# Decode attention of two caches on one core: the loads and units of the windowed cache, from four heads in 16 KB rows to eight heads in 32 KB rows

## The chip, the core and the metric

One core of one Trainium2 chip runs the kernel as one program. The metric is the device time in microseconds, the median of three runs. Beside it stands one execution that the hardware profiler recorded; its span runs from the first to the last instruction, and the durations in this document are those of that execution. The engines are called as in the profile: PE (matrix multiplication; PEld its weight loads), DVE (vector), ACT (scalar functions), POOL, and SP, whose instruction queue issues the loads. The loads themselves are carried out by the core's 16 DMA engines.

## What is computed

Two independent attention layers, A and B, each for one token with 32 query heads over 16 cached heads of 128 elements. B attends to all 8,192 cached keys, A only to the last 2,048 of them. Each has a query projection before and an output projection behind, and the two results stand side by side in the output.

```python
def _A_ref(x, k_cache, v_cache, wq, wo):
    W = min(4096, max(256, Sk // 4))          # 2048 of Sk = 8192; B takes all Sk
    rep = Hq // Hkv                            # 32 // 16
    q = (x @ wq).reshape(B, Sq, Hq, Dh).transpose(0, 2, 1, 3)
    k = jnp.repeat(k_cache[:, :, Sk - W:, :], rep, axis=1)
    v = jnp.repeat(v_cache[:, :, Sk - W:, :], rep, axis=1)
    scores = jnp.einsum("bhqd,bhkd->bhqk", q, k) * (Dh ** -0.5)
    p = _softmax(scores, axis=-1)
    o = jnp.einsum("bhqk,bhkd->bhqd", p, v)
    return o.transpose(0, 2, 1, 3).reshape(B, Sq, Hq * Dh) @ wo
return jnp.concatenate([a, b], axis=-1)
```

All data are bfloat16. K and V of A are 8.4 MB each, of B 33.6 MB each; with wq and wo the kernel reads 102.76 MB.

## The kernel before

**Units.** The work runs in units of four cached heads (eight query heads): four units of A, then four of B, numbered 0 to 7. A unit's K is one block of 128 partitions, with a row of keys in each partition: in A 64 keys (`TA`, 16 KB), in B 256 keys (64 KB, loaded in two halves). A unit is worked on in slabs of 16 keys per partition (`SLAB`, 2,048 elements): four slabs in a unit of A (`NA`), sixteen in one of B (`NB`).

**Loads.** `load_kv` builds the loads of a unit. For A the source pattern at L222 and L223 reads, outermost first, 32 pieces of a head, then four heads, then a row, so that partition 4q + h holds piece q of head h. For B the source is a plain block of 128 rows. `place` gives each load the next piece of a ring of 144 KB per partition, and makes it wait for the last use of whatever stood there: a K slab's transpose (T) or a V slab's product (V). All loads are issued by SP, in this order: part of wo, wq in four loads of 64 rows, then K of unit 0, and after it by turns K of unit i and V of unit i-1, then the rest of wo. A waiting load holds up every load behind it. Loads of K and V of A are at L224, of B at L232, of wo at L245.

**Queries.** The query projection (L312) fills eight banks; ACT copies them out in two pieces each (L328), DVE transposes them (L332) and spreads them into two zero-filled operands: `za` for A (z0, L338) and `zb` for B (z1, L343), in which a window that moves by a few columns puts each slab's scores into rows of their own.

**Inside a unit.** `turn` transposes a K slab on DVE (T, L364) into one of three buffers; `score` multiplies it on PE (S, L381: four matmuls of 512 columns, all slabs into one bank). In A four heads share a bank, and a matmul of a small mask (`mkl`, `mkr`, L373) puts a very low number where a query meets another head's keys. Then follow the row maximum (`peak`, DVE L396, turned by PE L398), its spreading (`spread`, DVE L406 and L409, PE L411), the exponential (`expo`, ACT L417 and L420), the transpose of the probabilities (`turnp`: one instruction for A into `pta`, L428; four of 32 partitions for B into `pts`, L432), the product with V (`pv`, L445: four matmuls per slab, each into its own group of 32 output columns), a copy by ACT (`take`, L452) and the sum over the four groups on PE (`fold`, L461). The program is written out so that unit i+1's transposes and scores stand between the softmax steps of unit i, and PV of unit i behind the last score of unit i+1.

**End.** The sums of the exponentials are gathered (lsel, L496 and L499), the outputs divided, and the output projection (L525) runs over wo as it lands.

Of the kernel before, what the change touches and what calls it, by code (L numbers as in the profile page):

```python
# [22 lines left out]
NB = ROW // SLAB  # L23
TA = 4 * W_A // 128
NA = TA * DH // SLAB
W0 = 2 * (NB - 1)
ZW = 128 + W0
ZA = 128 + 24
BIG = 1e30
# [70 lines left out]
def bass_concat_heads__sliding_block_cached__gqa_block_cached__decode_kernel(nc, A_x, A_k_cache, A_v_cache, A_wq, A_wo,  # L100
# [20 lines left out]

    za = nc.alloc_sbuf_tensor("za", [128, NQ, 4, ZA], BF16)

    mkl = nc.alloc_sbuf_tensor("mkl", [4, 16, 4, 2], BF16)
    mkr = nc.alloc_sbuf_tensor("mkr", [4, 128, 4], BF16)
    mx = nc.alloc_sbuf_tensor("mx", [128, 8], F32)
    mr = nc.alloc_sbuf_tensor("mr", [128, 8], F32)

    pta = nc.alloc_sbuf_tensor("pta", [128, NA, 16, 8], BF16)
    rsa = nc.alloc_sbuf_tensor("rsa", [128, NQ], F32)  # L130
    clsa = nc.alloc_sbuf_tensor("clsa", [128, 8], F32)
    mexp = nc.alloc_sbuf_tensor("mexp", [1, 128], F32)
# [79 lines left out]
    kv_at = {}  # L212
    UNITS = [(side, u) for side in "AB" for u in range(NQ)]
    NU = len(UNITS)
    nslab = [NA if side == "A" else NB for side, _ in UNITS]

    def load_kv(kind, i):
        side, u = UNITS[i]
        c = (ks if kind == "K" else vs)["AB".index(side)]
        use = "T%d.%d" if kind == "K" else "V%d.%d"  # L220
        if side == "A":
            src = bass.AP(tensor=c.tensor, offset=c.offset + (4 * u * SK + SK - W_A) * DH,  # L222
                          ap=[[TA * DH, 32], [SK * DH, 4], [1, TA * DH]])  # L223
            kv_at[kind, i] = [place(TA * DH, [use % (i, NA - 1)], lambda e, t: e.dma_start(t, src), "%s%d.0" % (kind, i))]  # L224
            return
        rows = c[0, 4 * u:4 * u + 4, :, :].rearrange("h (q t) d -> (h q) (t d)", q=32)
        n = 2 if kind == "K" or i == NU - 1 else 1
        kv_at[kind, i] = []
        for half in range(n):
            src = rows[:, half * ROW // n:(half + 1) * ROW // n]  # L230
            kv_at[kind, i].append(place(ROW // n, [use % (i, (half + 1) * NB // n - 1)],
                                        lambda e, t, src=src: e.dma_start(t, src), "%s%d.%d" % (kind, i, half)))  # L232
# [40 lines left out]
    op("pool", lambda e: e.memset(zb[:], 0.0), name="zb0")  # L273
    op("pool", lambda e: e.tensor_copy(mkr[:], view(ident, 128, 0, [[0, 128], [1, 4]], 4)), deps=["ident"], name="mkr")
    op("pool", lambda e: e.memset(pts[:], 0.0), name="pts0")
# [15 lines left out]
    for k0 in range(0, KW, 4):  # L291
        n = min(4, KW - k0)
        for P in range(2):
# [7 lines left out]
       deps=["identf"], name="clsb")  # L301
    op("dve", lambda e: e.tensor_reduce(clsa[:], view(identf, 128, 0, [[1, 8], [8, 16]]), AX.X, ALU.add),
       deps=["identf"], name="clsa")
    op("dve", lambda e: e.tensor_reduce(sel[:], view(identf, 128, 0, [[1, 32], [32, 4]]), AX.X, ALU.add),
       deps=["identf"], name="sel")
    op("dve", lambda e: e.tensor_scalar(mkl[:], view(ident, 128, 0, [[0, 16], [1, 4], [0, 2]], 4), -1.0, BIG,
                                        ALU.add, ALU.mult), deps=["ident"], name="mkl")
# [13 lines left out]
    for n in range(8):  # L321
# [15 lines left out]
    for b in range(4):  # L337
        op("dve", lambda e, b=b: e.tensor_copy(  # L338
            view(za, NQ * 4 * ZA, ZA - 128 + 32 * b, [[4 * ZA, NQ], [2 * ZA, 2], [ZA, 2], [1, 8]], 32, 32 * b),
            view(ktb, KT, 0, [[1024, NQ], [64, 2], [1, 2], [128, 8]], 32, 32 * (b % 2))),  # L340
            deps=QT + ["za0"], name="z0.%d" % b)
# [25 lines left out]
    def score(i, s):  # L367
# [3 lines left out]
        def mm(e):  # L371
            if side == "A" and s == 0:
                e.matmul(bank[:, :], lhsT=mkl[:].rearrange("p a h r -> p (a h r)"),  # L373
                         rhs=mkr[:].rearrange("p q h -> p (q h)"), start=True, stop=False)
# [26 lines left out]
    def spread(i):  # L401
        A = UNITS[i][0] == "A"
        deps = ["mT%d" % i] + (["mx%d" % (i - 1), "bc%d" % (i - 1)] if i else [])
        rows = [[1, 8], [8, 16]] if A else [[32, 4], [1, 2], [2, 16]]
        out = mr[0:1, :] if A else mr[0:1, :].rearrange("p (b r) -> p b r", r=2)
        op("dve", lambda e: e.tensor_reduce(out, view(mb, 512, 0, rows, parts=1), AX.X, ALU.max), deps=deps,  # L406
           name="mr%d" % i)
        to, of = ([[8, 16], [1, 8]], [[0, 16], [1, 8]]) if A else ([[32, 4], [2, 16], [1, 2]], [[2, 4], [0, 16], [1, 2]])
        op("dve", lambda e: e.tensor_scalar(view(mexp, 128, 0, to, parts=1), view(mr, 8, 0, of, parts=1), -SCALE, None,  # L409
                                            ALU.mult), deps=["mr%d" % i], name="mx%d" % i)  # L410
        op("pe", lambda e: e.matmul(mb[:, 128:129], lhsT=mexp[0:1, :], rhs=onesf[0:1, 0:1], start=True, stop=True),  # L411
           deps=["mx%d" % i, "ones"], name="bc%d" % i)
# [11 lines left out]
    def turnp(i):  # L424
        side, _ = UNITS[i]
        deps = ["exp%d" % i, "pts0"] + (["V%d.%d" % (i - 1, nslab[i - 1] - 1)] if i else [])
        if side == "A":
            op("dve", lambda e: e.transpose(view(pta, NA * 128, 0, [[8, 16], [128, NA], [1, 8]]), psb[:, :]),  # L428
               deps=deps, name="PT%d" % i)
        else:  # L430
            for b in range(4):
                op("dve", lambda e, b=b: e.transpose(  # L432
                    view(pts, NB * 128, 2 * b, [[8, 16], [128, NB], [1, 2]], 32, 32 * b), psb[32 * b:32 * b + 32, :]),
                   deps=deps, name="PT%d" % i if b == 3 else None)

    def pv(i, s):
        src, landed = slab("V", i, s)

        def mm(e):
            for j in range(4):  # L440
                if UNITS[i][0] == "A":
                    lhsT = pta[:, s, 4 * j:4 * j + 4, :].rearrange("p t k -> p (t k)")
                else:
                    lhsT = view(pts, NB * 128, 128 * s + 32 * j, [[1, 32]])
                ins = e.matmul(vbank[i][32 * j:32 * j + 32, :], lhsT=lhsT, rhs=src[:, 512 * j:512 * j + 512],  # L445
                               start=(s == 0), stop=(s == nslab[i] - 1))
            return ins
# [7 lines left out]
    def fold(i):  # L455
        side, u = UNITS[i]
        c, at = (1, 8 * u) if side == "A" else (0, HQ + 8 * u)

        def mm(e):
            for t in range(4):  # L460
                ins = e.matmul(ob[:, at:at + 8], lhsT=xo[:, c, 128 * t:128 * t + 128], rhs=sel[:, 8 * t:8 * t + 8],  # L461
                               start=(t == 0), stop=(t == 3))
            return ins
        op("pe", mm, deps=["xo%d" % i, "sel"], name="O%d" % i)

# [3 lines left out]
    for i in range(NU):  # L469
# [26 lines left out]
    op("dve", lambda e: e.tensor_tensor(  # L496
        lsel[:, 0, :].rearrange("p (u m) -> p u m", m=8), rsa[:, :].unsqueeze(2).to_broadcast([128, NQ, 8]),
        view(clsa, 8, 0, [[0, NQ], [1, 8]]), ALU.mult), deps=["exp%d" % (NQ - 1), "clsa"], name="lselA")
    op("dve", lambda e: e.tensor_tensor(  # L499
# [18 lines left out]
    def final(P, c):  # L518
        k0, kk = sum(NWO[P][:c]), NWO[P][c]

        def mm(e):
# [6 lines left out]
            return ins  # L528
        op("pe", mm, deps=["wo%d.%d" % (P, c), "oP", "exp%d" % (NQ - 2)], name="F%d.%d" % (P, c))

# [43 lines left out]
```

## Time and profile before

| | |
|---|---|
| median of three runs | 246.06 us (245.97 to 246.1) |
| the profiled execution | 245.95 us, span 244.6 us |
| busiest engines | PE 168.2 us, DVE 124.7 us |
| SP's DMA queue | 102.76 MB, 98.1% of 16 engines' span |
| K transposes (L364) | 80 of 1.211 us mean |
| score matmuls (L381) | 256 for B of 0.425 us mean, 64 for A of 0.448 us mean |
| PV matmuls (L445) | 256 for B of 0.546 us mean, 64 for A of 0.382 us mean |
| granted PE clock, mean | 0.847 |

The profile gives busy time per engine; a busy time near the span means that the engine has no room left. Matmuls overlap, so the mean of one is longer than the pace at which they follow each other. For the DMA engines the profile gives packets, bytes and the share of the 16 engines' time that was filled. Windows of the profile give, for a stretch of time, the busy time of PE, PEld, DVE, ACT and POOL with counts in brackets, then the granted PE clock, the share of the DMA engines and GB/s.

### The profile page before, as it was taken

To read this page: it belongs to the slowest core of one execution; us is meant where nothing else is said; L and a number is where in the kernel's file an instruction comes from. 1 tells how busy PE (TensorE), PEld (TensorE's weight loads), DVE (VectorE), ACT (ScalarE), POOL (GpSimd) and SP (SyncE) were. 2 spreads that over 40 slices of the span, in tenths; PEclk is the share of its full clock that TensorE was granted. 3 is DMA by queue.
4 is the path that set the end of the run, shared out by engine and by line. 5 is a ranking of instruction groups with operands and counts; after the bars stand their busy time and mean duration, and the time that the engine had idled before them with its cause. 6 is when DMAs were issued, how large, how long until landed. Compare 5 with 4: busy or idle time off the path is not lost.

```text
span 244.6 us, 2224 instructions
## 1 busy us (share of the span) xinstructions
PE 168.2 (69%) x952; PEld 69.5 (28%) x952; DVE 124.7 (51%) x156; ACT 21.5 (9%) x54; POOL 8.1 (3%) x15
## 2 busy tenths in 40 slices
PE   0059692977887799669736569938197976654696
PEld 0024240322444222323112323203052322321453
DVE  0040026677688998899700679930369960130200
ACT  2200052001121100200000010000010000200000
POOL 8400000000000000000000000000000000000000
PEclk9999899579999999979968767997855995757769
DMA  7999899999999999998989999989999999999994
GB/s 279 429 486 435 367 431 429 429 429 437 434 439 434 425 437 445 429 490 386 482 375 429 429 485 396 461 370 429 426 482 418 439 423 402 431 430 426 422 412 190
DMA packets 4369, 102.90 MB, mean 421 GB/s; under 512 B 516, under 2 KB 648, under 8 KB 904
## 3 DMA queue, kind: packets, MB, share of 16 engines
q1 hardware_dynamic: 4356, 102.76, 98.1%
q8 instruction: 7, 0.11, 0.2%
q14 instruction: 2, 0.02, 0.0%
q10 hardware_dynamic: 4, 0.00, 0.0%
HBM read 102.76 MB, written 0.00 MB: 420 GB/s over the span
## 4 chain that ended last, share of the span: by engine, by line
DMA 61%; PE 21%; DVE 12%; ACT 2%; issue 2%; SPq 2%; DVEq 0%
DMA ring<-in_B_v_cache_dram 39%; DMA ring<-in_B_wo_dram 12%; DMA ring<-in_B_wq_dram 10%; DVE ktb L364 9%; PE vb L445 7%; PE qb L381 5%; PE sb L312 2%; ACT psb L420 1%; DVE pta L428 1%; PE ob L461 1%; PE vb L312 1%; PE qb L312 1%; PE sb L381 1%; SPq L201 1%; PE qb L373 1%
## 5 line engine op out<-in xcount | busy, mean ns | idle before, releaser
L364 DVE STREAM_TRANSPOSE ktb<-ring 128x1024 int32<-128x1024 int32 x80 | 92.8, 1211 | 28.2 <-DMA ring<-in_B_k_cache_dram 27.1
L381 PE MATMUL sb<-ktb,zb 128*128 128x512 bf16 x256 | 73.2, 425 | 23.2 <-DVE ktb L364 20.5
L381 PEld LDWEIGHTS sb<-ktb,zb 128*128 128x128 bf16 x256 | 22.8, 104 | 70.1 <-DVE ktb L364 45.4
L445 PE MATMUL vb<-ring,pts 128*32 128x512 bf16 x256 | 23.6, 546 | 20.6 <-DMA ring<-in_B_v_cache_dram 16.5
L381 PE MATMUL qb<-ktb,za 128*128 128x512 bf16 x64 | 19.3, 448 | 2.8 <-DVE ktb L364 2.8
L445 PEld LDWEIGHTS vb<-ring,pts 128*32 128x32 bf16 x256 | 8.5, 130 | 35.2 <-DMA ring<-in_B_v_cache_dram 18.7
L452 ACT ACTIVATE xo<-vb 128x512 f32<-128x512 f32 x8 | 4.8, 597 | 130.3 <-PE vb L445 130.3
L432 DVE STREAM_TRANSPOSE pts<-psb 32x512 bf16<-32x512 bf16 x16 | 11.3, 704 | 7.7 <-ACT psb L420 7.5
L332 DVE STREAM_TRANSPOSE ktb<-qsb 128x512 int32<-128x512 int32 x4 | 2.8, 711 | 21.8 <-ACT qsb L328 21.8
L461 PEld LDWEIGHTS ob<-sel,xo 128*128 128x128 f32 x64 | 10.0, 226 | 3.4 <-ACT xo L452 2.1
L312 PE MATMUL sb<-ring,xrep 128*128 128x512 bf16 x18 | 7.3, 546 | 5.3 <-DMA ring<-in_B_wq_dram 5.3
L525 PE MATMUL qb<-ring,oP 128*1 128x256 bf16 (+1 forms) x112 | 10.2, 326 | 0.5 <-DMA ring<-in_B_wo_dram 0.5
L461 PE MATMUL ob<-sel,xo 128*128 128x8 f32 x64 | 9.3, 273 | 1.2 <-ACT xo L452 1.2
L381 PEld LDWEIGHTS qb<-ktb,za 128*128 128x128 bf16 x64 | 6.2, 109 | 13.3 <-issue 5.7
L287 PE MATMUL sb<-onesb,xint 1*128 1x128 bf16 x8 | 1.1, 307 | 11.7 <-ACT xint L283 11.7
L525 PEld LDWEIGHTS qb<-ring,oP 128*1 128x1 bf16 x112 | 5.9, 90 | 4.8 <-DMA ring<-in_B_wo_dram 1.7
L539 DVE CAST outsb<-qb 1x256 bf16<-1x256 f32 x2 | 0.8, 420 | 12.1 <-PE qb L525 12.1
L505 DVE RECIPROCAL rl<-mb 128x64 f32<-128x64 f32 x1 | 0.6, 557 | 12.3 <-PE mb L502 12.3
L295 DVE TENSOR_SCALAR xrep<-sb,par 128x256 bf16<-128x256 f32 x4 | 1.7, 477 | 10.1 <-PE sb L287 10.1
L373 PE MATMUL qb<-mkr,mkl 4*128 4x512 bf16 x4 | 1.8, 439 | 7.2 <-DVE ktb L364 7.2
L406 DVE TENSOR_REDUCE mr<-mb 1x8 f32<-1x128 f32 x8 | 1.9, 241 | 9.4 <-PE mb L398 9.4
L396 DVE TENSOR_REDUCE mx<-qb 128x1 f32<-128x512 f32 x4 | 2.8, 692 | 6.3 <-PE qb L381 6.3
(70 smaller groups left out, 86.2 us busy)
## 6 DMA issues: line engine op xcount, KB each, us to landing
ring<-in_B_k_cache_dram SPq DMA_DIRECT2D x8, 4096.0 KB, 24.1
ring<-in_A_k_cache_dram SPq DMA_DIRECT2D x4, 2048.0 KB, 32.6
ring<-in_A_v_cache_dram SPq DMA_DIRECT2D x4, 2048.0 KB, 26.2
ring<-in_B_v_cache_dram SPq DMA_DIRECT2D x2, 4096.0 KB, 23.8
ring<-in_A_wo_dram SPq DMA_DIRECT2D x1, 3456.0 KB, 21.4
ring<-in_A_wq_dram SPq DMA_DIRECT2D x1, 2560.0 KB, 19.4
ring<-in_B_wq_dram SPq DMA_DIRECT2D x1, 2560.0 KB, 24.7
ring<-in_B_wo_dram SPq DMA_DIRECT2D x1, 2448.0 KB, 26.8
```

The lines of the kernel that those rows point to most:

```text
L201: return e.dma_start(bass.AP(tensor=ring, offset=P * RING + lo, ap=[[2 * RING, 64], [1, (k1 - k0) * w]]), src)
L312: return e.matmul(banks[n][:, :], lhsT=xrep[:, k, :], rhs=wq_at[k][:, n * 512:(n + 1) * 512], start=(k == 0), stop=(k == KW - 1))
L332: op("dve", lambda e, n=n: e.transpose(ktb[:, (n - 1) * 512:(n + 1) * 512].bitcast(I32), qsb[:, n - 1:n + 1, :].rearrange("p a n -> p (a n ...
L364: op("dve", lambda e: e.transpose(kt.bitcast(I32), src.bitcast(I32)), deps=[landed] + (["S%d" % (k - NKT)] if k >= NKT else Z), name="T%d. ...
L373: e.matmul(bank[:, :], lhsT=mkl[:].rearrange("p a h r -> p (a h r)"), rhs=mkr[:].rearrange("p q h -> p (q h)"), start=True, stop=False)
L381: ins = e.matmul(bank[:, :], lhsT=lhsT, rhs=view(ktb, KT, (k % NKT) * SLAB + 64 * c + v, [[128, 16], [2, 32]]), start=(side == "B" and s = ...
L396: op("dve", lambda e: e.tensor_reduce(mx[:, 0:1], sbank[i][:, :], AX.X, ALU.max), deps=["S%d" % (k0[i] + nslab[i] - 1)] + (["mT%d" % (i - ...
L432: op("dve", lambda e, b=b: e.transpose(view(pts, NB * 128, 2 * b, [[8, 16], [128, NB], [1, 2]], 32, 32 * b), psb[32 * b:32 * b + 32, :]), ...
L445: ins = e.matmul(vbank[i][32 * j:32 * j + 32, :], lhsT=lhsT, rhs=src[:, 512 * j:512 * j + 512], start=(s == 0), stop=(s == nslab[i] - 1))
L452: op("act", lambda e: e.activation(xo[:, c, :], vbank[i][:, :], ACT.Copy), deps=["V%d.%d" % (i, nslab[i] - 1)] + (["O%d" % (i - 1)] if i e ...
L461: ins = e.matmul(ob[:, at:at + 8], lhsT=xo[:, c, 128 * t:128 * t + 128], rhs=sel[:, 8 * t:8 * t + 8], start=(t == 0), stop=(t == 3))
L525: ins = e.matmul(fb[r:r + 1, 0:hi - lo], lhsT=oP[:, P, k0 + k:k0 + k + 1], rhs=wo_at[P, c][:, k * DM + lo:k * DM + hi], start=(k0 + k == 0 ...
```

## The change

A now runs in two units of eight cached heads instead of four units of four, so there are six units. A row in a partition holds 128 keys of a head (32 KB); the source pattern reads, outermost first, eight heads, then 16 pieces, then a row, so that partition 16h + q holds piece q of head h. There are four loads of 4 MB for K and V of A instead of eight of 2 MB, and eight slabs in a unit of A. The number of K transposes, score and PV matmuls stays the same. Half of the scores of a bank are masked (two heads share a group of 32 partitions), the mask has two rows instead of four. A's probabilities are now transposed in four parts like B's, into a `pta` that POOL clears first; PV of A writes two groups of 64 columns, each group twice per slab; the fold sums over two groups with a wider selection (`sela`). On the way, z1 moves from DVE to ACT in eight small copies, and the first two banks of queries are copied out in four pieces each. The diff, cut:

```diff
-TA = 4 * W_A // 128
+HA = 8
+UA = G // HA
+TA = HA * W_A // 128
 NA = TA * DH // SLAB
...
-ZA = 128 + 24
+RA = 2 * HA // 4
+WA = RA * (NA - 1)
+ZA = 128 + WA
...
-    UNITS = [(side, u) for side in "AB" for u in range(NQ)]
+    UNITS = [(side, u) for side in "AB" for u in range(UA if side == "A" else NQ)]
...
-            src = bass.AP(tensor=c.tensor, offset=c.offset + (4 * u * SK + SK - W_A) * DH,
-                          ap=[[TA * DH, 32], [SK * DH, 4], [1, TA * DH]])
+            src = bass.AP(tensor=c.tensor, offset=c.offset + (HA * u * SK + SK - W_A) * DH,
+                          ap=[[SK * DH, HA], [TA * DH, 128 // HA], [1, TA * DH]])
...
+    op("pool", lambda e: e.memset(pta[:], 0.0), name="pta0")
...
+    op("dve", lambda e: e.tensor_reduce(sela[:], view(identf, 128, 0, [[1, 8 * HA], [8 * HA, 2]]), AX.X, ALU.add),
+       deps=["identf"], name="sela")
...
-        for h in range(2):
-            op("act", lambda e, n=n, h=h: e.activation(qsb[:, n, 256 * h:256 * h + 256],
-                                                       banks[n][:, 256 * h:256 * h + 256], ACT.Copy),
-               deps=["qmm%d" % (KW0 + n)], name="qe%d" % n if h else None)
+        cut = 128 if n < 2 else 256
+        for lo in range(0, 512, cut):
+            op("act", lambda e, n=n, lo=lo, cut=cut: e.activation(qsb[:, n, lo:lo + cut], banks[n][:, lo:lo + cut],
+                                                                  ACT.Copy),
+               deps=["qmm%d" % (KW0 + n)], name="qe%d" % n if lo + cut == 512 else None)
...
     for b in range(4):
-        op("dve", lambda e, b=b: e.tensor_copy(
-            view(zb, NQ * 4 * ZW, 32 * b + W0, [[4 * ZW, NQ], [2 * ZW, 2], [ZW, 2], [1, 2]], 32, 32 * b),
-            view(ktb, KT, b * 256, [[1024, NQ], [64, 2], [1, 2], [128, 2]], 32, 64 + 32 * (b % 2))),
-            deps=QT + ["zb0"], name="z1.%d" % b)
+        for c in range(2):
+            op("act", lambda e, b=b, c=c: e.activation(
+                view(zb, NQ * 4 * ZW, 32 * b + W0 + 2 * ZW * c, [[4 * ZW, NQ], [ZW, 2], [1, 2]], 32, 32 * b),
+                view(ktb, KT, b * 256 + 64 * c, [[1024, NQ], [1, 2], [128, 2]], 32, 64 + 32 * (b % 2)), ACT.Copy),
+                deps=QT + ["zb0"], name="z1.%d" % b if c else None)
...
                     if side == "A":
-                        lhsT = za[:, u, 2 * c + v, ZA - 128 - 8 * s:ZA - 8 * s]
+                        lhsT = za[:, u, 2 * c + v, WA - RA * s:WA - RA * s + 128]
...
-        if side == "A":
-            op("dve", lambda e: e.transpose(view(pta, NA * 128, 0, [[8, 16], [128, NA], [1, 8]]), psb[:, :]),
-               deps=deps, name="PT%d" % i)
-        else:
-            for b in range(4):
...
+        t, n, m = (pta, NA, RA) if side == "A" else (pts, NB, 2)
+        for b in range(4):
+            op("dve", lambda e, b=b: e.transpose(
+                view(t, n * 64 * m, m * b, [[4 * m, 16], [64 * m, n], [1, m]], 32, 32 * b), psb[32 * b:32 * b + 32, :]),
+               deps=deps, name="PT%d" % i if b == 3 else None)
...
-                    lhsT = pta[:, s, 4 * j:4 * j + 4, :].rearrange("p t k -> p (t k)")
+                    lhsT, w, g = pta[:, s, 4 * j:4 * j + 4, :].rearrange("p t k -> p (t k)"), 8 * HA, 2
...
-                ins = e.matmul(vbank[i][32 * j:32 * j + 32, :], lhsT=lhsT, rhs=src[:, 512 * j:512 * j + 512],
-                               start=(s == 0), stop=(s == nslab[i] - 1))
+                ins = e.matmul(vbank[i][w * (j % g):w * (j % g) + w, :], lhsT=lhsT, rhs=src[:, 512 * j:512 * j + 512],
+                               start=(s == 0 and j < g), stop=(s == nslab[i] - 1 and j >= 4 - g))
```

More of the change, by code (lines that the diff above doesn't have):

```diff
@@ L120, in bass_concat_heads__sliding_block_cached__gqa_block_cached__decode_kernel @@
     zb = nc.alloc_sbuf_tensor("zb", [128, NQ, 4, ZW], BF16)
-    za = nc.alloc_sbuf_tensor("za", [128, NQ, 4, ZA], BF16)
-    mkl = nc.alloc_sbuf_tensor("mkl", [4, 16, 4, 2], BF16)
-    mkr = nc.alloc_sbuf_tensor("mkr", [4, 128, 4], BF16)
+    za = nc.alloc_sbuf_tensor("za", [128, UA, 4, ZA], BF16)
+    mkl = nc.alloc_sbuf_tensor("mkl", [2, 32, 2, 2], BF16)
+    mkr = nc.alloc_sbuf_tensor("mkr", [2, 16, 2, 16], BF16)
     mx = nc.alloc_sbuf_tensor("mx", [128, 8], F32)
[L127 to L131, printed above, removed]
+    mr = nc.alloc_sbuf_tensor("mr", [128, 2 * HA], F32)
+    pta = nc.alloc_sbuf_tensor("pta", [128, NA, 16, 2 * HA], BF16)
+    rsa = nc.alloc_sbuf_tensor("rsa", [128, UA], F32)
+    clsa = nc.alloc_sbuf_tensor("clsa", [128, 2 * HA], F32)
     mexp = nc.alloc_sbuf_tensor("mexp", [1, 128], F32)
@@ L139, in bass_concat_heads__sliding_block_cached__gqa_block_cached__decode_kernel @@
     sel = nc.alloc_sbuf_tensor("sel", [128, 32], F32)
+    sela = nc.alloc_sbuf_tensor("sela", [128, 8 * HA], F32)
     par = nc.alloc_sbuf_tensor("par", [128, 2], F32)
@@ L273, in bass_concat_heads__sliding_block_cached__gqa_block_cached__decode_kernel @@
     op("pool", lambda e: e.memset(zb[:], 0.0), name="zb0")
-    op("pool", lambda e: e.tensor_copy(mkr[:], view(ident, 128, 0, [[0, 128], [1, 4]], 4)), deps=["ident"], name="mkr")
+    op("pool", lambda e: e.tensor_copy(mkr[:], view(ident, 128, 0, [[0, 16], [1, 2], [0, 16]], 2)), deps=["ident"],
+       name="mkr")
+    op("pool", lambda e: e.memset(pta[:], 0.0), name="pta0")
     op("pool", lambda e: e.memset(pts[:], 0.0), name="pts0")
@@ L301, in bass_concat_heads__sliding_block_cached__gqa_block_cached__decode_kernel @@
        deps=["identf"], name="clsb")
-    op("dve", lambda e: e.tensor_reduce(clsa[:], view(identf, 128, 0, [[1, 8], [8, 16]]), AX.X, ALU.add),
+    op("dve", lambda e: e.tensor_reduce(clsa[:].rearrange("p (b r) -> p b r", r=RA),
+                                        view(identf, 128, 0, [[32, 4], [1, RA], [RA, NA]]), AX.X, ALU.add),
        deps=["identf"], name="clsa")
+    op("dve", lambda e: e.tensor_reduce(sela[:], view(identf, 128, 0, [[1, 8 * HA], [8 * HA, 2]]), AX.X, ALU.add),
+       deps=["identf"], name="sela")
     op("dve", lambda e: e.tensor_reduce(sel[:], view(identf, 128, 0, [[1, 32], [32, 4]]), AX.X, ALU.add),
        deps=["identf"], name="sel")
-    op("dve", lambda e: e.tensor_scalar(mkl[:], view(ident, 128, 0, [[0, 16], [1, 4], [0, 2]], 4), -1.0, BIG,
+    op("dve", lambda e: e.tensor_scalar(mkl[:], view(ident, 128, 0, [[0, 32], [1, 2], [0, 2]], 2), -1.0, BIG,
                                         ALU.add, ALU.mult), deps=["ident"], name="mkl")
@@ L338, in bass_concat_heads__sliding_block_cached__gqa_block_cached__decode_kernel @@
         op("dve", lambda e, b=b: e.tensor_copy(
-            view(za, NQ * 4 * ZA, ZA - 128 + 32 * b, [[4 * ZA, NQ], [2 * ZA, 2], [ZA, 2], [1, 8]], 32, 32 * b),
-            view(ktb, KT, 0, [[1024, NQ], [64, 2], [1, 2], [128, 8]], 32, 32 * (b % 2))),
+            view(za, UA * 4 * ZA, WA + 32 * b, [[4 * ZA, UA], [2 * ZA, 2], [ZA, 2], [1, RA]], 32, 32 * b),
+            view(ktb, KT, RA * DH * b, [[2 * HA * DH, UA], [64, 2], [1, 2], [128, RA]], 32, 32 * (b % 2))),
             deps=QT + ["za0"], name="z0.%d" % b)
     for b in range(4):
-        op("dve", lambda e, b=b: e.tensor_copy(
-            view(zb, NQ * 4 * ZW, 32 * b + W0, [[4 * ZW, NQ], [2 * ZW, 2], [ZW, 2], [1, 2]], 32, 32 * b),
-            view(ktb, KT, b * 256, [[1024, NQ], [64, 2], [1, 2], [128, 2]], 32, 64 + 32 * (b % 2))),
-            deps=QT + ["zb0"], name="z1.%d" % b)
+        for c in range(2):
[3 more added lines that the diff above has]
+                deps=QT + ["zb0"], name="z1.%d" % b if c else None)
     Z = ["%s.%d" % (z, b) for z in ("z0", "z1") for b in range(4)]
@@ L373, in mm @@
                 e.matmul(bank[:, :], lhsT=mkl[:].rearrange("p a h r -> p (a h r)"),
-                         rhs=mkr[:].rearrange("p q h -> p (q h)"), start=True, stop=False)
+                         rhs=mkr[:].rearrange("p t h g -> p (t h g)"), start=True, stop=False)
             for c in range(2):
@@ L403, in spread @@
         deps = ["mT%d" % i] + (["mx%d" % (i - 1), "bc%d" % (i - 1)] if i else [])
-        rows = [[1, 8], [8, 16]] if A else [[32, 4], [1, 2], [2, 16]]
-        out = mr[0:1, :] if A else mr[0:1, :].rearrange("p (b r) -> p b r", r=2)
+        m, n = (RA, NA) if A else (2, NB)
+        out = mr[0:1, 0:4 * m].rearrange("p (b r) -> p b r", r=m)
+        rows = [[32, 4], [1, m], [m, n]]
         op("dve", lambda e: e.tensor_reduce(out, view(mb, 512, 0, rows, parts=1), AX.X, ALU.max), deps=deps,
            name="mr%d" % i)
-        to, of = ([[8, 16], [1, 8]], [[0, 16], [1, 8]]) if A else ([[32, 4], [2, 16], [1, 2]], [[2, 4], [0, 16], [1, 2]])
-        op("dve", lambda e: e.tensor_scalar(view(mexp, 128, 0, to, parts=1), view(mr, 8, 0, of, parts=1), -SCALE, None,
+        to, of = [[32, 4], [m, n], [1, m]], [[m, 4], [0, n], [1, m]]
+        op("dve", lambda e: e.tensor_scalar(view(mexp, 128, 0, to, parts=1), view(mr, 2 * HA, 0, of, parts=1), -SCALE, None,
                                             ALU.mult), deps=["mr%d" % i], name="mx%d" % i)
@@ L425, in turnp @@
         side, _ = UNITS[i]
-        deps = ["exp%d" % i, "pts0"] + (["V%d.%d" % (i - 1, nslab[i - 1] - 1)] if i else [])
-        if side == "A":
-            op("dve", lambda e: e.transpose(view(pta, NA * 128, 0, [[8, 16], [128, NA], [1, 8]]), psb[:, :]),
-               deps=deps, name="PT%d" % i)
-        else:
-            for b in range(4):
-                op("dve", lambda e, b=b: e.transpose(
-                    view(pts, NB * 128, 2 * b, [[8, 16], [128, NB], [1, 2]], 32, 32 * b), psb[32 * b:32 * b + 32, :]),
-                   deps=deps, name="PT%d" % i if b == 3 else None)
+        deps = ["exp%d" % i, "pts0", "pta0"] + (["V%d.%d" % (i - 1, nslab[i - 1] - 1)] if i else [])
+        t, n, m = (pta, NA, RA) if side == "A" else (pts, NB, 2)
[3 more added lines that the diff above has]
+               deps=deps, name="PT%d" % i if b == 3 else None)
     def pv(i, s):
@@ L441, in mm @@
                 if UNITS[i][0] == "A":
-                    lhsT = pta[:, s, 4 * j:4 * j + 4, :].rearrange("p t k -> p (t k)")
+                    lhsT, w, g = pta[:, s, 4 * j:4 * j + 4, :].rearrange("p t k -> p (t k)"), 8 * HA, 2
                 else:
-                    lhsT = view(pts, NB * 128, 128 * s + 32 * j, [[1, 32]])
-                ins = e.matmul(vbank[i][32 * j:32 * j + 32, :], lhsT=lhsT, rhs=src[:, 512 * j:512 * j + 512],
-                               start=(s == 0), stop=(s == nslab[i] - 1))
+                    lhsT, w, g = view(pts, NB * 128, 128 * s + 32 * j, [[1, 32]]), 32, 4
+                ins = e.matmul(vbank[i][w * (j % g):w * (j % g) + w, :], lhsT=lhsT, rhs=src[:, 512 * j:512 * j + 512],
+                               start=(s == 0 and j < g), stop=(s == nslab[i] - 1 and j >= 4 - g))
             return ins
@@ L456, in fold @@
         side, u = UNITS[i]
-        c, at = (1, 8 * u) if side == "A" else (0, HQ + 8 * u)
+        c, at, n, pick = (1, 2 * HA * u, 2 * HA, sela) if side == "A" else (0, HQ + 8 * u, 8, sel)
         def mm(e):
             for t in range(4):
-                ins = e.matmul(ob[:, at:at + 8], lhsT=xo[:, c, 128 * t:128 * t + 128], rhs=sel[:, 8 * t:8 * t + 8],
+                ins = e.matmul(ob[:, at:at + n], lhsT=xo[:, c, 128 * t:128 * t + 128], rhs=pick[:, n * t:n * t + n],
                                start=(t == 0), stop=(t == 3))
             return ins
-        op("pe", mm, deps=["xo%d" % i, "sel"], name="O%d" % i)
+        op("pe", mm, deps=["xo%d" % i, "sel", "sela"], name="O%d" % i)
     for s in range(nslab[0]):
@@ L496, in bass_concat_heads__sliding_block_cached__gqa_block_cached__decode_kernel @@
     op("dve", lambda e: e.tensor_tensor(
-        lsel[:, 0, :].rearrange("p (u m) -> p u m", m=8), rsa[:, :].unsqueeze(2).to_broadcast([128, NQ, 8]),
-        view(clsa, 8, 0, [[0, NQ], [1, 8]]), ALU.mult), deps=["exp%d" % (NQ - 1), "clsa"], name="lselA")
+        lsel[:, 0, :].rearrange("p (u m) -> p u m", m=2 * HA), rsa[:, :].unsqueeze(2).to_broadcast([128, UA, 2 * HA]),
+        view(clsa, 2 * HA, 0, [[0, UA], [1, 2 * HA]]), ALU.mult), deps=["exp%d" % (UA - 1), "clsa"], name="lselA")
     op("dve", lambda e: e.tensor_tensor(
@@ L528, in mm @@
             return ins
-        op("pe", mm, deps=["wo%d.%d" % (P, c), "oP", "exp%d" % (NQ - 2)], name="F%d.%d" % (P, c))
+        op("pe", mm, deps=["wo%d.%d" % (P, c), "oP", "exp%d" % (UA - 2)], name="F%d.%d" % (P, c))
     for P in range(2):
```

## The prediction

> **What bounds the kernel now.** I read the page from the top: busy shares and slices, then the DMA queues, then the mean rates of three stretches, then the DMA issues, and last SP's own order of time.
>
> ```profile
> PE 168.2 (69%) x952; PEld 69.5 (28%) x952; DVE 124.7 (51%) x156; ACT 21.5 (9%) x54; POOL 8.1 (3%) x15
> DMA  7999899999999999998989999989999999999994
> DMA packets 4369, 102.90 MB, mean 421 GB/s; under 512 B 516, under 2 KB 648, under 8 KB 904
> q1 hardware_dynamic: 4356, 102.76, 98.1%
> q10 hardware_dynamic: 4, 0.00, 0.0%
> ```
>
> No engine is busy over 69% of the span, while SP's queue (q1) holds the 16 DMA engines for 98.1% of it: 240.0 of 244.6 us. The only empty stretches are the start and the end. So the time is the time of a stream of 102.76 MB, and an edit to PE, DVE or ACT counts only if it starves that stream.
>
> ```profile
> 28.00:62.00 34.00, 26.16 (x105) 9.87 (x105) 19.11 (x30) 6.81 (x20) 0.00 (x0) 0.80 1.01 432
> 62.00:81.00 19.00, 15.29 (x105) 7.80 (x105) 14.32 (x19) 4.04 (x11) 0.00 (x0) 1.00 1.00 427
> 125.00:242.00 117.00, 81.48 (x552) 35.46 (x553) 49.83 (x59) 5.66 (x14) 0.00 (x0) 0.76 0.99 426
> ```
>
> The last number of each line is GB/s, the one before it the share of the DMA engines. A's K and V load in the first stretch (seven of the eight 2 MB loads), B's K in the second, V, K and wo in the third. A's 16 KB rows run at the same rate as B's 32 and 64 KB rows, 427 to 432 GB/s, or 27 GB/s per DMA engine. The trace's record of single packets gives the same as durations (means): 0.617 us for a row of 16 KB (1,024 of them, half at 0.611), 1.218 us for 32 KB, 2.423 us for 64 KB.
>
> ```profile
> ring<-in_A_k_cache_dram SPq DMA_DIRECT2D x4, 2048.0 KB, 32.6
> ring<-in_B_v_cache_dram SPq DMA_DIRECT2D x2, 4096.0 KB, 23.8
> 74.33 12.91 SPq L232 DMA_DIRECT2D ring<-in_B_k_cache_dram  x2
> 98.02 0.33 SPq L232 DMA_DIRECT2D ring<-in_B_v_cache_dram  x1
> ```
>
> Loads land 20 to 40 us after their issue because others are queued ahead. The tightest place is the first load of B's V: it waits for A's last PV and goes out at 98.0 us, while the K half issued at 86.9 us lands 20.1 us later, at 107.0. Compute could be 9.0 us later there before the stream would run dry.
>
> **How many DMA engines a load uses.** This is the part of the change that matters. The loads of before are 3,840 rows, the two output stores two more, and q1 has 4,356 packets: 514 are left, the small ones of the page's "under 512 B". The 32 loads at 16 each and the two stores at one each are exactly 514: each DMA engine that takes part in a transfer ends it with one small write. All loads, whose source patterns count 32, 64 or 128 in their outermost dimension, ran on 16 engines; the stores and the two x loads (q10: two rows and two small writes) count one there and ran on one. A's source pattern of before is 32 groups of 4 heads. The new one is 8 heads of 16 rows. The rows allow two readings: engines follow the destination's 128 partitions (16), or they are the outermost count of the narrower side, at most 16 (8). Between the counts seen, 1 and 32, I take the second, since a transfer cut along its outermost loop has only eight pieces. [...]
>
> **The change part by part.**
>
> 1. A's loads. Before: 8 loads of 128 rows of 16 KB, 64 rows per DMA engine, 64 × 0.617 = 39.5 us of each engine's stream. After: 4 loads of 128 rows of 32 KB. On eight engines that is 64 rows of 32 KB for each of those, and none for the other eight. Every later load waits on the slower half, since it needs all its pieces, so the loaded engines set the end. Price of a row: the lower bound is B's 1.218 us, so 64 × 1.218 = 78.0 us, 38.5 more than before. The upper bound is a row that gets only half of its path: the nearest row is V's 64 KB, 2.423 us for twice the bytes through one place, so 64 × 2.423 = 155.1 us, 115.6 more.
>  I take the upper end. Engine h then holds head h and writes partitions 16h to 16h+15 one after the other, all eight beginning together, with sources exactly 2 MB apart; before, the 32 outer groups let neighbouring engines stand 16 KB apart in the source and four partitions apart in the destination. All loads of before are spread in that way, so their common 27 GB/s does not tell whether an engine or the place it writes to sets it; bunching is what this layout does to the latter. [...]
>
> 2. Waits of the stream. Eight engines idle while the loaded ones work, and run ahead into B's first K halves, 8 rows of each per load. That writes into partitions that A's rows also want: between 0 and two such loads in the way, 2 × 8 × 1.218 = 19.5 us; I take 5. SP's order is otherwise as before: from the first B load on the same bytes stand ahead of each load and the same uses free the ring. A's loads take more room (32 KB of 144 per partition), so V of unit 0 now waits for the first qmm's (25.7 us in SP's order of before), with some 2 × 20 us of K queued ahead.
>
> 3. Compute, all under the stream. The rows are these, of the costliest groups and, the last, of the order of time:
>
> ```profile
> L432 DVE STREAM_TRANSPOSE pts<-psb 32x512 bf16<-32x512 bf16 x16 | 11.3, 704 | 7.7 <-ACT psb L420 7.5
> L428 DVE STREAM_TRANSPOSE pta<-psb 128x512 bf16<-128x512 bf16 x4 | 2.8, 712 | 3.5 <-ACT psb L420 3.5
> L445 PE MATMUL vb<-ring,pta 128*32 128x512 bf16 x64 | 4.2, 382 | 0.0
> 58.50 1.05 PE L445 MATMUL vb<-ring,pta 128*32 128x512 bf16 x16
> ```
>
>  P transposes: 8 × 0.704 = 5.6 us (the four-part kind, pts) for 4 × 0.712 = 2.8, +2.8 on DVE. Two units fewer: 2 × (0.69 + 0.24 + 0.21) = 2.3 less on DVE, 2 × 0.95 of fold and 2 masks of 0.44 less on PE. PV: 64 matmuls before and after, 16 in 1.05 us with four groups; two groups make 16 in 2.1, 64 in 8.4 for 4.2, +4.2 (bounds: 0, and one by one at 0.382, 24.4, +20). z1 goes to ACT: eight small copies at 0.17 to 0.21 are 1.5 us beside DVE's four z0 (0.17 each at a quarter of the elements), so the first K transpose starts at 41.8 for 42.1. ACT's extra qsb cuts are of the first two banks and end before the last bank does. POOL's memset of pta is as big as that of pts, 1.8 us, 30 us before its use. In all at most some +5 us ahead of the load that has 9.0 us of cover; with A's loads slower still, DVE and PE wait for them and the cover grows. Without cover it would cost the excess over 9.0.
>
> Sum, against the profiled execution's 245.95 us (span 244.6 and 1.35 around it; the median of the runs is 246.06): 245.95 − 39.5 + 155.1 + 5 = **366 us**.
>
> **The rivals.**
>
> *Eight engines, rows at full speed.* For it: in all 1,408 rows of 32 KB nothing but scattered outliers goes beyond 1.24 us, so an engine's own rate may be the limit. Against it: no load of before bunches its writers. 245.95 − 39.5 + 78.0 = 284.4 us. [...]
>
> *Sixteen engines, not slower.* Place: the split of A's four loads over the engines. If it follows the 128 partitions, nothing is lost and each engine has 32 rows at 1.218 = 39.0 for 39.5 us: 245.4 us. It decides from the point where the small writes number 450 (28 × 16 + 2) and not 418. For it: all loads of before, also those of 64 rows, had 16; against it: none had an outermost count under 16 but those with one.
>
> *PV or DVE starves the stream with sixteen engines.* PV one by one, +20 us, all of it ahead of the tight load: 245.4 + (20 + 2.8 − 9.0), up to 259 us. Against it: the groups overlap fourfold today.
>
> **How the numbers follow.** Eight engines with rows lengthened by 0.3 to 1.1 of a row: 0.80, 308 to 382 us, most likely 366; eight engines at full speed or near it: 0.13, 284; sixteen: 0.05, 245.4, half of it beyond 0.2% and half within; starved with sixteen: 0.02, 259. The range is 308 to 382: 1.3 rows (64 × 1.583 = 101.3, 308) to twice with all 19.5 us of collisions (381). Two in ten lie outside, most of it at 284. About 0.2%, 0.5 us, is what a measurement of this kernel can tell from no change. Faster 0.025, same 0.025, slower 0.95.
>
> **What would show it.** q1 with 3,748 packets (3,330 rows and 418 small writes) means eight engines, 3,780 sixteen. The first A load, issued at 3.8 us and landing near 37 in before's place for the same bytes, lands near 67 if rows are doubled, near 47 if not. The DMA share in A's stretch falls from 1.0 to about a half, at 110 GB/s if doubled and 215 if not (plus what the other eight take ahead). DVE's waits for in_A_k_cache and PE's for in_A_v_cache, none on the page of before, would be the longest. Wrong would be: a full DMA row in A's stretch; a stream that runs dry in B's stretch as well; or rows of 1.2 us with the end beyond 300 us, which would make item 2 the cost.

## The result, and the profile after

| | before | after |
|---|---|---|
| median of five runs | 246.06 us | 388.95 us (388.77 to 389.99) |
| the profiled execution | 245.95 us, span 244.6 | 389.99 us, span 388.6 |
| after / before | | 1.582 (1.580 to 1.584) |

The change makes the kernel 142.9 us slower; 366 was forecast. First the slices of the page (40 of 9.7 us) and its queue line:

```profile
DMA  8994998559985555478799448999999999999983
GB/s 338 418 381 91 162 162 135 108 110 148 148 135 108 108 108 108 128 297 328 137 162 159 84 148 327 445 396 422 449 442 413 425 445 447 411 425 431 418 357 128
q1 hardware_dynamic: 3748, 102.76, 82.4%
```

The 3,748 packets are 3,330 rows and the 418 small writes that belong to eight engines per load of A. From the fourth slice to the 24th the rate is mostly 84 to 162 GB/s, where it was 427 to 432 before. Yet some of these slices are at 5 tenths and others at 8 or 9: two regimes, both at a low rate. Three windows show them cleanly (the last two numbers: share of the DMA engines, GB/s):

```profile
40.00:62.00 22.00, 0.00 (x0) 0.00 (x0) 0.68 (x4) 1.26 (x8) 0.00 (x0) 0.57 0.98 143
120.00:155.00 35.00, 12.66 (x35) 4.22 (x35) 13.15 (x15) 0.95 (x3) 0.00 (x0) 0.65 0.52 110
240.00:290.00 50.00, 35.48 (x162) 14.78 (x162) 30.22 (x34) 2.50 (x7) 0.00 (x0) 0.69 0.99 428
```

At 120 to 155 us eight engines work and eight stand idle. At 40 to 62 us all sixteen are busy, and move 143 GB/s against 110. From 240 us on, in B alone, the stream is what it was. The record of single packets gives the three as durations of a 32 KB row: 2.49 us with eight engines at work (in a pattern 2.55, 2.55, 2.55, 2.3), 3.3 to 3.65 us with sixteen, and 1.21 us in B alone. SP's order of time (start, us, instruction) says when sixteen are busy:

```profile
38.51 48.88 SPq L237 DMA_DIRECT2D ring<-in_B_k_cache_dram  x2
138.30 0.63 SPq L229 DMA_DIRECT2D ring<-in_A_v_cache_dram  x1
169.97 18.40 SPq L237 DMA_DIRECT2D ring<-in_B_k_cache_dram  x2
```

The first line is both halves of the K of unit 2, one issued at 38.5 us and one at 87.1. Rows of 3.3 to 3.65 us stand at 40 to 66 us and at 88 to 115, thus from each issue on; and again at 188 to 216, after the second half of unit 3 (issued at 188.1). They are B rows that the eight free engines carry out ahead of their turn, and A rows of the loaded engines beside them.

The waits of DVE and PE (us in total, times, longest), and four steps of the chain:

```profile
DVE ktb L376 <- DMA ring<-in_B_k_cache_dram: 99.8, 4, 42.0
DVE ktb L376 <- DMA ring<-in_A_k_cache_dram: 71.1, 2, 35.6
PE vb L455 <- DMA ring<-in_A_v_cache_dram: 56.5, 2, 33.3
```

```profile
41.42 34.92 another core or an unknown queue
76.36 1.26 DVE ktb L376
88.87 35.47 another core or an unknown queue
141.01 31.99 another core or an unknown queue
```

Compute waits for A's loads, and for B's K, whose rows stand behind A's on the loaded engines. The chain can't name these waits ("unknown queue": each of the three pieces ends as a K block lands, the first two A's, the third B's). The first K transpose starts at 76.4 us; it was 42.1.

### The profile page after: what moved, and what is told of

Same layout as the page of the kernel before. It is cut to its first block, busy times and chain, and to the rows that moved or that the text cites. A ratio compares the mean times of both kernels' runs of the same rounds, so it can differ in the third digit from the quotient of the medians.

```text
span 388.6 us, 2157 instructions
## 1 busy us (share of the span) xinstructions
PE 180.8 (47%) x925; PEld 73.7 (19%) x926; DVE 125.0 (32%) x151; ACT 20.0 (5%) x58; POOL 8.9 (2%) x16
## 3 DMA queue, kind: packets, MB, share of 16 engines
q1 hardware_dynamic: 3748, 102.76, 82.4%
## 4 chain that ended last, share of the span: by engine, by line
DMA 40%; another core or an unknown queue 35%; PE 15%; DVE 7%; ACT 1%; SPq 1%; issue 1%; DVEq 0%
DMA ring<-in_B_v_cache_dram 25%; DMA ring<-in_B_wo_dram 8%; DMA ring<-in_B_wq_dram 6%; PE vb L455 6%; DVE ktb L376 5%; PE qb L393 4%; DVE pta L442 1%; PE sb L322 1%; PE qb L322 1%; PE sb L393 1%; PE vb L322 1%; SPq L206 0%; ACT psb L433 0%; PE ob L471 0%
## 5 line engine op out<-in xcount | busy, mean ns | idle before, releaser
L376 DVE STREAM_TRANSPOSE ktb<-ring 128x1024 int32<-128x1024 int32 x80 | 92.6, 1213 | 172.6 <-DMA ring<-in_B_k_cache_dram 99.8
L393 PE MATMUL sb<-ktb,zb 128*128 128x512 bf16 x256 | 77.8, 445 | 27.9 <-DVE ktb L376 25.2
L455 PE MATMUL vb<-ring,pta 128*64 128x512 bf16 x64 | 13.0, 597 | 56.5 <-DMA ring<-in_A_v_cache_dram 56.5
L385 PE MATMUL qb<-mkr,mkl 2*128 2x512 bf16 x2 | 1.2, 602 | 75.5 <-DVE ktb L376 75.5
L393 PE MATMUL qb<-ktb,za 128*128 128x512 bf16 x64 | 21.6, 506 | 2.0 <-DVE ktb L376 1.9
L455 PEld LDWEIGHTS vb<-ring,pta 128*64 128x64 bf16 x64 | 5.3, 168 | 64.3 <-DMA ring<-in_A_v_cache_dram 57.5
L462 ACT ACTIVATE xo<-vb 128x512 f32<-128x512 f32 x6 | 3.6, 597 | 199.5 <-PE vb L455 199.5
L322 PE MATMUL sb<-ring,xrep 128*128 128x512 bf16 x17 | 5.8, 455 | 7.0 <-DMA ring<-in_B_wq_dram 6.7
L442 DVE STREAM_TRANSPOSE pta<-psb 32x512 bf16<-32x512 bf16 x8 | 5.6, 702 | 3.8 <-ACT psb L433 3.7
L471 PEld LDWEIGHTS ob<-sel,xo 128*128 128x128 f32 x32 | 5.8, 262 | 3.0 <-ACT xo L462 2.3
L471 PE MATMUL ob<-sel,xo 128*128 128x8 f32 x32 | 5.5, 301 | 1.2 <-ACT xo L462 1.2
```

The costliest lines, as they stand in the source:

```text
L322: return e.matmul(banks[n][:, :], lhsT=xrep[:, k, :], rhs=wq_at[k][:, n * 512:(n + 1) * 512], start=(k == 0), stop=(k == KW - 1))
L376: op("dve", lambda e: e.transpose(kt.bitcast(I32), src.bitcast(I32)), deps=[landed] + (["S%d" % (k - NKT)] if k >= NKT else Z), name="T%d. ...
L393: ins = e.matmul(bank[:, :], lhsT=lhsT, rhs=view(ktb, KT, (k % NKT) * SLAB + 64 * c + v, [[128, 16], [2, 32]]), start=(side == "B" and s = ...
L442: op("dve", lambda e, b=b: e.transpose(view(t, n * 64 * m, m * b, [[4 * m, 16], [64 * m, n], [1, m]], 32, 32 * b), psb[32 * b:32 * b + 32, ...
L455: ins = e.matmul(vbank[i][w * (j % g):w * (j % g) + w, :], lhsT=lhsT, rhs=src[:, 512 * j:512 * j + 512], start=(s == 0 and j < g), stop=(s ...
L462: op("act", lambda e: e.activation(xo[:, c, :], vbank[i][:, :], ACT.Copy), deps=["V%d.%d" % (i, nslab[i] - 1)] + (["O%d" % (i - 1)] if i e ...
```

## The experiments

Each edit is against the changed kernel. The first was run eleven times and the kernel with both waits twice, the others once; the kernel before, run beside them, stayed between 245.94 and 246.3 us. A "place" below stands for partitions that by the row times do not take two writers at full speed: four neighbours (sixteen pieces of one partition each, side by side, have rows of 4.3 to 4.4 us) and the four that lie 32 away within the same half of the 128 (four pieces 32 apart begin with rows of 2.5 us, about twice and not four times the 1.21 us of eight pieces that begin four partitions apart). It is the author's reading of these times, and no run separates it from other groupings. "Writers of a place" are the engines whose rows go there at one time. The trace names neither the engine nor the partition of a row: both are inferred from the patterns and the times.

### Is it the load's pattern, and nothing of the compute?

```diff
-                          ap=[[SK * DH, HA], [TA * DH, 128 // HA], [1, TA * DH]])
+                          ap=[[TA * DH, 32], [SK * DH, 4], [1, TA * DH]])
```

> The changed kernel with A's source pattern as before the change: 32 outer groups of four heads, rows of 32 KB kept (it reads 128 keys per row in 32 rows of four heads, so A's half of the output is computed from other data). All other parts of the change stay: two units of eight, masks, two PV groups, P transposes in four parts, z1 on ACT. Both theories: 16 engines, 3,780 packets, rows of 1.22 us, no stretch with a DMA share under 0.9; 245.4 us, that is 0.998 of before, since 64 rows of 0.617 us become 32 of 1.218 us and compute stays hidden. If some of the compute edits cost time by themselves, it would be above 246.6 us.

245.78 us, 0.9988 of before (0.9979 to 0.9997). Its queue line, and the window of A's stretch and of B's first K:

```profile
q1 hardware_dynamic: 3780, 102.76, 98.0%
```

```profile
34.00:81.00 47.00, 35.05 (x150) 14.04 (x149) 35.17 (x42) 7.10 (x25) 0.00 (x0) 0.84 1.01 433
```

With 32 outer steps the 32 KB rows, the units of eight heads, the masks, the transposes in four parts and PV in two groups add nothing to the time: the whole 143 us belong to the source pattern of four loads. Of the remaining arithmetic one group, PV of A (mean ns of one), first in the changed kernel and then here:

```profile
L455 PE MATMUL vb<-ring,pta 128*64 128x512 bf16 x64 | 13.0, 597 | 56.5 <-DMA ring<-in_A_v_cache_dram 56.5
```

```profile
L455 PE MATMUL vb<-ring,pta 128*64 128x512 bf16 x64 | 7.3, 380 | 0.0
```

The same 64 matmuls take 13.0 us where PE stands idle for A's V before them, and 7.3 where they never wait. A longer mean of one matmul is here a result of the slow stream, not a cause: after the idle time the granted clock is low (0.54 at 160 to 170 us in the changed kernel, against 0.84 in the window above).

### Do the sources 2 MB apart matter?

```diff
-                          ap=[[SK * DH, HA], [TA * DH, 128 // HA], [1, TA * DH]])
+                          ap=[[17 * TA * DH, HA], [TA * DH, 128 // HA], [1, TA * DH]])
```

> The changed kernel with one number altered: in A's loads the eight outer blocks lie 17 rows (544 KB) apart in the source and no longer 2 MB; engines (eight), destination partitions and row size stay. A then reads other keys of its caches, so its half of the output is computed from other data. Theory 'destination' (two writers bunched in the same place of the partitions double a row's time, a third writer triples it): nothing changes, 389 us within 1%, 3,748 packets, DMA share near 0.5 at about 108 GB/s while only A loads. Theory 'source' (eight streams exactly 2 MB apart get in each other's way in HBM): rows fall to about 1.22 us and the time to 245.95 - 39.5 + 78.0 = 284 us.

389.23 us, 3,748 packets and much the same pattern of rows: with the sources 544 KB apart the time is that of 2 MB (388.95 us).

### Or the destinations?

```diff
+                src = bass.AP(tensor=c.tensor, offset=c.offset + (HA * u * SK + SK - W_A) * DH + 4 * j * TA * DH,
+                              ap=[[SK * DH, HA], [TA * DH, 4], [1, TA * DH]])
+                return e.dma_start(bass.AP(tensor=ring, offset=32 * j * RING + lo, ap=[[RING, 32], [1, TA * DH]]), src)
...
+            for j in range(parts):
```

> The opposite alteration: still eight engines with one head each, sources still 2 MB apart and rows of 32 KB, but each A load is cut into four loads of 32 partitions (outer count 8, four rows of each head per load), so that the eight engines write eight neighbouring groups of four partitions and not the starts of eight blocks of 16. The keys of A's heads stand in other partitions than the scores assume, so A's half of the output is not the reference's. Theory 'destination': rows at about 1.22 us, 284 us. Theory 'source': as the changed kernel, 366 to 389 us. Both: A's loads on eight engines; small writes 24 x 16 + 16 x 8 + 2 = 514, so 3,844 packets.

307.25 us. Still eight engines and sources 2 MB apart, but A's rows take 1.21 us when alone, half of the change's. Two windows, A alone and then B's rows beside A's:

```profile
28.00:38.00 10.00, 9.95 (x39) 4.17 (x40) 2.13 (x3) 4.86 (x18) 0.00 (x0) 0.84 0.51 220
44.00:50.00 6.00, 0.00 (x0) 0.00 (x0) 0.00 (x0) 0.00 (x0) 0.00 (x0) 0.50 1.02 218
```

Rows of 2.43 to 2.55 us, of A and B alike, stand only where B's rows run ahead while A's load writes the upper half of the partitions (the third and fourth of its four parts); beside A's lower half both kinds take 1.21. If the rows run ahead go to the upper half, a row doubled here where two engines write the same place (2.43 to 2.55 us against 1.21).

Then the other direction, a count of 16 with a bunched destination (partition 8q + h):

```diff
-                          ap=[[SK * DH, HA], [TA * DH, 128 // HA], [1, TA * DH]])
+                          ap=[[TA * DH, 16], [SK * DH, 8], [1, TA * DH]])
```

> The changed kernel with A's source pattern as 16 outer pieces of eight heads (partition 8q + h), outer count 16. A's scores then meet other heads' keys than they assume, so A's half of the output is not the reference's. Engines: all 16 (3,780 packets). If the loads are cut into blocks of eight partitions, engines whose blocks are 32 partitions apart stand in the same place, two writers each as in the changed kernel: 32 rows of 2.49 us, 245.95 - 39.5 + 79.7 = 286 us. If the number of engines alone counted, 245.5 us.

289.39 us. The window of A's stretch:

```profile
50.00:70.00 20.00, 9.35 (x35) 3.15 (x34) 8.84 (x9) 0.00 (x0) 0.00 (x0) 0.76 1.01 209
```

Sixteen engines, all busy, and half the rate: rows of 2.52 us, near the 286 us expected of two writers. This is the trap of the profile's page: a full DMA row that moves half the bytes. And one load per head, sixteen engines within 16 partitions:

```diff
+                src = bass.AP(tensor=c.tensor, offset=c.offset + ((HA * u + j) * SK + SK - W_A) * DH,
+                              ap=[[TA * DH, 128 // HA], [1, TA * DH]])
+                return e.dma_start(bass.AP(tensor=ring, offset=16 * j * RING + lo, ap=[[RING, 16], [1, TA * DH]]), src)
```

> The same placement as in the changed kernel, but each A load issued as eight loads of one head (16 partitions, outer count 16), so all 16 engines take part, two rows of each engine per 4 MB less than before per engine: 32 rows per engine in all. The result is that of the reference. Theory 'destination': sixteen writers stand in one block of 16 partitions, twice as bunched as the eight were in pairs, four to a place: rows of about 4 x 1.22 us, A in 32 x 4.87 = 156 us, 245.95 - 39.5 + 156 = 362 us. Theory 'source' (and theory 'only the number of engines counts'): rows at about 1.22 us and 246 us. Packets 3,330 + 24 x 16 + 32 x 16 + 2 - 2 = about 4,226.

346.66 us, in A's stretch

```profile
50.00:100.00 50.00, 10.51 (x35) 3.52 (x35) 11.15 (x10) 0.00 (x0) 0.00 (x0) 0.60 0.97 116
```

with rows of 4.3 to 4.4 us there (3.6 times 1.21) and mostly 4.05 to 4.2 in V1. Four writers of a place cost a little less than four times; why less stays open. The last of these patterns has four outer steps:

```diff
-                          ap=[[SK * DH, HA], [TA * DH, 128 // HA], [1, TA * DH]])
+                          ap=[[2 * SK * DH, 4], [TA * DH, 32], [1, TA * DH]])
```

> The changed kernel with A's source pattern as four outer blocks of 32 rows (outer count 4; it reads 32 rows of four heads 4 MB apart, so A's half of the output is computed from other data). If engines follow the outer count: four engines, small writes 24 x 16 + 4 x 4 + 2 = 402, 3,732 packets; four writers at the starts of blocks of 32 partitions, in pairs at the same place, 128 rows of 2.49 us on each: 245.95 - 39.5 + 318.7 = 525 us, and up to 35 more for the B loads that run ahead. If engines followed the destination's partitions or stopped at eight, 389 us or less.

482.35 us and 3,732 packets, thus four engines. The expectation of 525 missed: the rows begin at 2.5 us, then every fourth shortens step by step, and from 180 us on more than half of the rows (B's among them) are under 2.1 us. Why they shorten was not shown. In the changed kernel the rows hardly shorten: every fourth goes from 2.33 us to 2.22 by 154 us.

### What are the missing 22 us?

```diff
+        deps += {"K2.0": ["K0.0", "K1.0", "V0.0"], "K3.0": ["V1.0"]}.get(name, [])
```

Two waits on SP let B's K halves out only when A's loads have landed.

> The changed kernel with two waits added on SP: the first load of B's unit 2 waits until K0, K1 and V0 have landed, the first load of unit 3 until V1 has landed, so that the eight engines without A rows can't run ahead. Theory 'a third writer': rows of A stay at about 2.49 us instead of up to 3.65, so 245.95 - 39.5 + 64 x 2.49 = 366 us, and some 4 us for the two gaps in the stream: 370 us, 19 us less than the changed kernel although waits were added. Theory 'A's rows are that slow whoever else runs': no gain, and the waits cost, 390 to 400 us.

366.5 us, 1.490 of before (1.485 to 1.494). Two more waits make the kernel 22.4 us faster. A stretch that had sixteen busy engines now has eight:

```profile
40.00:60.00 20.00, 0.00 (x0) 0.00 (x0) 0.00 (x0) 0.00 (x0) 0.00 (x0) 0.50 0.49 105
```

A's 64 rows take 153.8 us on each loaded engine, 2.40 each: three of four take 2.45 to 2.55 us, and every fourth 2.15, falling to about 1.6 at the end of V1. In the changed kernel the 64 rows take 182.8 us.

The same two waits on the spread loads:

> spread8 (eight engines, destinations spread) with the same two waits. With nothing running ahead every row should take 1.21 us: 245.95 - 39.5 + 64 x 1.218 + 4 = 288 us, against 307.25 without the waits; hardly any row over 1.6 us (325 of 1,920 in spread8). If the slow rows of spread8 had another cause, it stays at 307 or above. A's half of the output is computed from keys in other places, as in spread8.

289.96 us, with 31 rows over 1.6 us against 325:

```profile
50.00:70.00 20.00, 10.82 (x38) 3.47 (x35) 10.66 (x12) 0.00 (x0) 0.00 (x0) 0.76 0.51 220
```

Eight engines at full row speed are 220 GB/s at half the share. This is the first rival, made: 284.4 by its sum.

Then each wait alone:

> Only the first of the two waits is left: K2's halves go out when K0, K1 and V0 have landed, K3's may run ahead during V1. If the 22.4 us between the changed kernel (388.95) and the one with both waits (366.5) come from all four run-ahead loads alike, each pair costs about 11 us and this is near 378 us, with long rows (about 3.6 us) in V1's stretch alone. If only the pair during K0 and K1 costs, which is where the prediction stopped counting, it is near 366; if only the later pair, near 389. Packets as before, 3,748.

> Only the second wait is left: K3's halves go out when V1 has landed, K2's run ahead during K0 and K1. By all four loads alike near 378 us, with long rows in the first stretch alone; 389 if only the first pair costs, 366 if only the second. What this run and the one with the first wait alone cost beyond 366.5 should add up to about 22 us.

385.04 us with the first wait alone, 380.21 with the second alone: 18.5 and 13.7 over 366.5. Each pair of halves costs. In the first, the rows beside V1 are long from 168 to 220 us:

```profile
172.00:216.00 44.00, 10.61 (x41) 3.07 (x40) 11.03 (x11) 0.00 (x0) 0.00 (x0) 0.69 0.98 144
```

V1 has 16 rows on each loaded engine, as many as the two halves have on each free one; 16 × (3.6 − 2.4) = 19 us, against 18.5. For the second wait alone the same sum is too high for the 13.7 measured: there the 48 rows of K0, K1 and V0 take 132.1 us against 117.0, and every fourth of those without a collision shrinks to 1.8 us. The two do not add up to 22 as expected but to 32, because in the changed kernel only three of the four halves collide: in the packets, the first half of unit 3 (issued at 170.0) passes at 1.21 us beside unit 2's own B rows, before V1 begins. Three halves are 24 rows on each free engine, and A's rows take 182.8 − 153.8 = 29.0 us longer, 1.2 us for each. The time agrees: the changed kernel stands 28.7 us over the sum without collisions, 245.95 − 39.5 + 153.8 = 360.25. The kernel with both waits stands 6.3 us over that sum. Most of this are the gaps that its waits leave: at each wait the packets show about 2 us without a row and first rows of 1.4 to 2.4 us, and the slice before the V load at 145.9 us fell to 75 GB/s.

### Must the rows share a place?

```diff
+                src = bass.AP(tensor=c.tensor, offset=c.offset + (HA * u * SK + SK - W_A) * DH + 8 * j * TA * DH,
+                              ap=[[SK * DH, HA], [TA * DH, 8], [1, TA * DH]])
+                return e.dma_start(bass.AP(tensor=ring, offset=64 * j * RING + lo, ap=[[RING, 64], [1, TA * DH]]), src)
```

> Each A load is cut into two loads of 64 partitions, eight heads of 8 rows each, so that piece h writes partitions 8h to 8h+7 of its half, first the lower half of the partitions, then the upper. Eight engines, two writers per place as in the change (pieces h and h+4 stand 32 apart), so A's rows alone stay near 2.45 us. B's run-ahead rows go to partitions 64 to 127. If rows slow each other only where they share a place, the run-ahead rows take 1.22 us and A's 2.45 while A writes the lower half, and all are longer only while it writes the upper one: about half of the 22.4 us remain, near 378 us. If a doubled-up place slows every engine that works beside it, rows are near 3.6 us for both in either half: near 389 us. If pieces 8 apart don't meet, rows are 1.22 us and the time is near 300. A's data stand in other partitions than its scores and PV expect.

379.65 us. First a window where A writes the lower half, then one of the upper:

```profile
38.00:45.00 7.00, 0.39 (x2) 0.00 (x0) 1.44 (x5) 1.98 (x11) 0.00 (x0) 0.74 1.08 225
52.00:60.00 8.00, 0.00 (x0) 0.00 (x0) 0.00 (x0) 0.00 (x0) 0.00 (x0) 0.50 0.91 131
```

The time is as the place theory had it, and the theory by which every engine always slows (389) falls: in the lower half A's rows stay at 2.55 us and lose nothing. But the rows run ahead were expected at 1.22 there and took 2.55 too. The row times met in these runs, 1.21, 2.5 and 3.6 us, are one, two and three times a row, and fit a third reading: all engines at work keep the pace of the place with the most writers, which is two for A alone and three where rows run ahead into a pair. The changed kernel fits it too: four of its eight heads lie in the lower half, where by the place alone rows should have stayed at 2.5 us, and yet all sixteen engines take 3.3 to 3.65. No run separates this from other couplings, and the rows of four engines that shorten from 2.5 to under 2.1 us and the 4.4 us of four writers stand against it as a strict law. What couples the engines stays open.

## Why the prediction was right and wrong

- *Number of engines*: right. The packet count forecast for eight engines was met to the packet, and in the other patterns four outer steps gave four engines (3,732 packets), 16 and 32 gave sixteen (a DMA share of 1.01 in A's stretch).
- *Price of an A row* (item 1): right, and the bunched writers are what lengthens it. 64 × 2.423 = 155.1 was forecast by the nearest row; with B held back the loaded engines have 153.8. That the two agree within 1% is partly luck: no row is steadily twice 1.21, but three of four are longer (2.45 to 2.55) and every fourth is shorter (2.15 to 1.6). No run behind the forecast shows a row that gets half of its path, as the 155.1 supposes; what the later ones show is 2.49 us with eight bunched engines, 2.52 with sixteen in blocks of eight partitions, and 1.21 with eight spread out.
- *Compute hidden* (item 3): right, with sixteen engines too. The third rival, PV starving the stream, is out: PV of A took 7.3 us undisturbed, 8.4 forecast.
- *Waits of the stream* (item 2): this step failed, in its size. "Between 0 and two such loads in the way, 2 × 8 × 1.218 = 19.5 us; I take 5." The price of a row was good (1.2 us each), but the 5 had no row behind it, and two was the wrong count: three halves of 8 rows per free engine collide, one of them beside V1, and nearly every such row counts in full. The step measures 29.0 us in A's rows and 28.7 in time; against the kernel that holds B back it is 22.4, since that one pays 6.3 for its waits. With 153.8 and 29.0 in place of 155.1 and 5, the forecast's own sum (366.55 as written) gives 389.3, against 388.95. The upper end of the range was built on the same count of two and fell short by 7 us.
- Of the signs, the packets, the DMA share of a half and 110 GB/s came as forecast. The first load was to land near 67 us if rows are doubled. That failed by item 2 too: the first transpose starts at 76.4 us, and at 67.3 in the kernel that holds B back. "A full DMA row in A's stretch" was named as a sign of being wrong and appeared (0.98 at 40 to 62 us), from the rows run ahead. DVE waits longest in total for B's K (99.8 us) and not for A's (71.1).
- The rival of eight engines at full row speed (284.4) exists as a kernel (289.96), but the change's layout does not give it.

Of the kernels that put A's data where its scores and PV expect them, the kernel before stays the fastest: the changed layout is at best 346.66 us with a load per head, and 366.5 with B held back. The 245.78 us above belong to a pattern that reads other keys; no run looked for one that both puts eight heads of 16 rows in their places and spreads its writers.

## What to carry to other kernels

Count the outermost steps of a load's source pattern before bytes or rows: here four steps ran on four DMA engines, eight on eight, 16 and 32 on all sixteen, and the count of small packets showed it (402 with four, 418 with eight, 450 with 32). Then ask where in the partitions these engines write at the same time: pieces four partitions apart ran at full row speed here (1.21 us), pieces 8, 16 or 32 apart at about half (2.52 to 2.55, 2.49 and, at first, 2.5 us), and pieces of one partition each, side by side, at about a quarter (4.3 to 4.4 us). A queue that leaves engines free lets later loads run ahead, and those are not free of cost: where they meet the late load's rows, holding them back was faster here (366.5 us against 388.95).

## What was not expected of the hardware

- Rows that run ahead on idle engines slow the late ones: 2.45 to 3.6 us for all sixteen engines, 143 GB/s with sixteen busy against 110 with eight. Loads of one core slow each other here, and no run shows by what mechanism.
- A DMA share of 0.97 to 1.01 says nothing of the rate: 433, 209, 143 and 116 GB/s were all seen at it.
- Where two engines write a place, the rows stay long for tens of rows. With eight engines and B held back three of four rows take 2.45 us or more over all 64, and only every fourth shortens; with four engines the rows shorten further, to 1.21 us for some.
